# The last layer of a fused attention, expert and token-mixing kernel: token rows gathered as 512-byte quarters and transposed by VectorE, with GpSimd's elementwise work there given to VectorE

## The chip, the core and the metric

The kernel runs on one NeuronCore of a Trainium2 chip. The metric is the device time of one execution in microseconds (us). A core has TensorE (matrix products; PE and, for its weight loads, PEld in the profile), VectorE (DVE), ScalarE (ACT), GpSimd (POOL) and SyncE (SP, which here issues transfers). Each engine works through its own queue in order and waits on semaphores of the others. On-chip memory is SBUF and, for matrix results, PSUM; both have 128 partitions.

## What is computed

Three stages: attention with a local window, a mixture of 8 experts, and a last layer that mixes channels and tokens. Only the last one is changed in its working; the experts' output rows change their order of columns.

```
# last layer: x is (2, 768, 512), the output of the experts
theta = x @ w_theta
zr, zi = x * cos(theta), x * sin(theta)
y = w_tok_r @ zr + w_tok_i @ zi          # over the 768 tokens, for each batch element
u = x + y
out = u + max(u @ w_ch, 0)
```

## The kernel before

All products of the last layer are made of three passes: an operand is split into a high part, rounded for TensorE's faster 32-bit form (`F32R`), and the rest, and high by high, high by low and low by high are added in PSUM.

The experts (the loop over `u`, lines 1630 to 1724) write weighted rows to a table `yd` in device memory, in the order of expert slots: `y_rows` and `y_head` with ScalarE, `y_last` with VectorE, `y_few` with ScalarE. `first_put` builds block 0 of the next layer's transposed input by TensorE out of gathered rows and the last expert's rows.

The last layer (from line 1727) goes through 12 blocks of 128 tokens, 6 for each batch element. For block `k` these steps exist:

- `gather_y(k)` (L1736): GpSimd issues one indirect transfer that fetches the 128 rows, 2 KB each, into a tile `yg` (tokens on partitions). Four such buffers exist.
- `h_tr(k)` (L1747): TensorE transposes the four 128 by 128 squares into PSUM (tile `b`).
- `h_xh` (L1754) and `h_xf` (L1761): ScalarE copies that to `xh` (high part) and to `xTf`, the full transposed input that `u = x + y` needs at the end. `h_xl` (L1767): VectorE makes the low part `xl`.
- `h_theta(k)` (L1783): 12 matmuls of `xh` and `xl` with `wth`, into `th`.
- `trig_a` (L1793 to L1801): ScalarE and VectorE bring `th` into the range of the sine; `trig_s` (L1808 to L1810): ScalarE makes sin and, by half the angle squared, cos.
- `trig_b`: `si * x` on GpSimd (L1815), and on VectorE `kk = 1 - 2 kk` (L1821) and `kk * x` (L1822), with `x` the gathered rows.
- `trig_c`: ScalarE makes the high parts `z` (L1834); the low part of the sine side on GpSimd, of the cosine side on VectorE (both L1839). Block 0 and 1 use VectorE for all of it.
- `h_mix(k, d)` for d = 0 to 3 (L1859): 12 matmuls each, `z` with the token weights `wtok`/`wtokr`, summed over blocks into `a`.

The order is written out by hand: round `k` of the loop at line 1992 issues mix(k,0), gather(k+4), theta(k+2), transpose(k+3), mix(k,1), then trig_a(k+2) with the high and low part of x(k+3), trig_s, mix(k,2), trig_b, mix(k,3), trig_c. So TensorE is two blocks behind the gathering and one ahead in theta. Between these steps `job_tick` slips in pieces of a decoding job for weights (L401 to L414, ScalarE and VectorE); the last of 26 such jobs falls in round 7. At the end of a batch element (k = 5 and 11) `h_u` (L1871, L1878) adds the mixed sums to `xTf`, `h_split` (L1885, L1886) splits the result, with two of the four low parts of the first element on GpSimd, and `h_out` (L1896, L1904) makes the output.

Of the kernel before, what the change touches and what calls it, by code (L numbers as in the profile page):

```python
# [48 lines left out]
YLAST = RBASE[E - 1] * 128  # L49
NRAW = 3  # L50
# [35 lines left out]
HU = 32  # L86
XL = 0
# [8 lines left out]
def f32(ap):  # L96
    return ap.bitcast(F32)


@with_exitstack  # L100
def kernel(
# [93 lines left out]
    yidx = ct([128, NB], I32, "yidx")  # L195
    erows = {}
# [249 lines left out]
    with ExitStack() as actx:  # L446
# [338 lines left out]
        def lead_out():  # L785
            A.activation(y0, head["y"], AF.Copy)
# [582 lines left out]
    with ExitStack() as mctx:  # L1369
# [14 lines left out]

        def gather_p0():
            pslot[0] = mb.tile([128, 1], F32, tag="ps", name="ps", bufs=6)
            G.indirect_dma_start(pslot[0], None, pd[:], bass.IndirectOffsetOnAxis(ap=prow[:, 24:25], axis=0))
# [167 lines left out]
        def mm2_few(u, out=None):  # L1555
# [4 lines left out]
            for v in (u, u + 1):  # L1560
                hx, w = fews.pop(v)
                for g in range(128 // c if c < 128 else 0):
# [3 lines left out]
                        rhs=w[:, 4 * g * c : 4 * (g + 1) * c],  # L1566
# [22 lines left out]
        def y_rows(r, lo, hi):  # L1589
            for i in range(lo, hi):  # L1590
# [6 lines left out]
                A.activation(yo[:P, :W], yp[:P, :W], AF.Copy, scale=ps)  # L1597
# [13 lines left out]
        def y_few():  # L1611
# [8 lines left out]
            A.activation(yo, out[:, :W], AF.Copy, scale=pslot.pop(RBASE[E - 1] + 1))  # L1620
# [9 lines left out]
        for u in range(64):  # L1630
# [79 lines left out]
            if 0 <= i < RTILES[r]:  # L1710
                gather_p(r, i)
            if u == HU:
# [14 lines left out]
    with ExitStack() as hctx:  # L1727
        hb = hctx.enter_context(tc.tile_pool(name="hb", bufs=2, side="right", reuse_waits="tile"))
        pA = hctx.enter_context(tc.tile_pool(name="pA", bufs=6, space=PSUM))
        x2s, xTb, zs, xps, xparts, ths, trig, acc, us = {}, {}, {}, {}, {}, {}, {}, {}, {}  # L1730
# [7 lines left out]

        def h_tr(k, pool=None):
# [3 lines left out]
            if t == 0:  # L1743
                xTb[b] = hb.tile([128, 4, S], F32, tag="xTf", name="xTf")
            tp = (pool or pB).tile([128, 4, 128], F32, tag="a" if pool else "b", name="b")
            for j in range(4):
                PE.transpose(tp[:, j], x2s[k][:, j * 128 : (j + 1) * 128], ident)  # L1747
            xps[k] = tp

        def h_xh(k, both=True):  # L1750
# [5 lines left out]
            if both:  # L1756
# [28 lines left out]
        def trig_a(k, c=slice(0, DM), tick=lambda: None):  # L1785
# [9 lines left out]
            V.tensor_scalar(kk, kk, MAGIC, None, op0=ALU.subtract)  # L1795
# [16 lines left out]
        def trig_i(k, c=slice(0, DM), eng=G):  # L1812
            if k < NB:
                si = trig[k][2][:, c]
                eng.tensor_tensor(si, si, x2s[k][:, c], op=ALU.mult)  # L1815

        def trig_r(k, c=slice(0, DM)):
            if k >= NB:
                return
            kk, x2 = trig[k][0][:, c], x2s[k][:, c]  # L1820
            V.tensor_scalar(kk, kk, -2.0, 1.0, op0=ALU.mult, op1=ALU.add)  # L1821
            V.tensor_tensor(kk, kk, x2, op=ALU.mult)  # L1822

        def trig_b(k, c=slice(0, DM), eng=G):
# [16 lines left out]
        def trig_c(k, c=slice(0, DM), eng=G):  # L1841
# [145 lines left out]
        gather_y(4)  # L1987
# [4 lines left out]
        for k in range(1, NB):  # L1992
# [10 lines left out]
            gather_y(k + 4)  # L2003
# [12 lines left out]
            if k == HS:  # L2016
                h_split(0, 0, 0, S)
                h_split(0, 1, 0, S, G)
# [10 lines left out]
            if k == HS:  # L2029
                h_split(0, 2, 0, S)  # L2030
                h_split(0, 3, 0, S, G)
# [72 lines left out]
```

## Time and profile before

| | us |
|---|---|
| median of the 3 runs (474.62 to 477.23) | 474.84 |
| the profiled execution's own time | 472.97 |
| its span, first to last instruction | 471.2 |
| TensorE busy in the span | 462.9 (98%) |
| VectorE busy | 349.4 (74%) |
| ScalarE busy | 254.3 (54%) |
| GpSimd busy | 134.0 (28%) |

[...] The last layer lies between about 292 us and the end. The profile's views are: busy time by stretch, groups of instructions by line, the timeline, and the chain of work that ended last. In the timeline two instructions of one engine may overlap, since the next one starts while the one before drains.

### The profile page before, as it was taken

To read this page: it belongs to the slowest core of one execution; us is meant where nothing else is said; L and a number is where in the kernel's file an instruction comes from. 1 tells how busy PE (TensorE), PEld (TensorE's weight loads), DVE (VectorE), ACT (ScalarE), POOL (GpSimd) and SP (SyncE) were. 2 spreads that over 40 slices of the span, in tenths; PEclk is the share of its full clock that TensorE was granted. 3 is DMA by queue.
4 is the path that set the end of the run, shared out by engine and by line. 5 is a ranking of instruction groups with operands and counts; after the bars stand their busy time and mean duration, and the time that the engine had idled before them with its cause. 6 is when DMAs were issued, how large, how long until landed. Compare 5 with 4: busy or idle time off the path is not lost.

```text
span 471.2 us, 9456 instructions
## 1 busy us (share of the span) xinstructions
PE 462.9 (98%) x3310; PEld 382.6 (81%) x3310; DVE 349.4 (74%) x918; ACT 254.3 (54%) x613; POOL 134.0 (28%) x185
## 2 busy tenths in 40 slices
PE   8999999999999999999999999999999999999996
PEld 4677777788888898878777888888888888888885
DVE  5888889778678687878887746587999899751522
ACT  5988786722647666565754544556555355520300
POOL 8602322204041403040514302104543332430400
PEclk9999999999999999999999999999999999999999
DMA  8977577616967888888999991600023000001022
GB/s 243 370 226 255 166 250 248 231 47 197 323 181 232 281 292 272 256 255 275 310 348 298 304 321 61 207 24 22 24 73 125 12 19 19 1 33 35 34 79 93
DMA packets 60490, 82.97 MB, mean 176 GB/s; under 512 B 5608, under 2 KB 39656, under 8 KB 60440
## 3 DMA queue, kind: packets, MB, share of 16 engines
q1 hardware_dynamic: 52212, 62.06, 40.3%
q0 software_dynamic: 4272, 9.92, 6.7%
q10 hardware_dynamic: 3956, 10.36, 6.6%
q8 instruction: 27, 0.44, 0.4%
q14 instruction: 23, 0.19, 0.1%
HBM read 70.94 MB, written 11.38 MB: 175 GB/s over the span
## 4 chain that ended last, share of the span: by engine, by line
PE 86%; ACT 4%; DMA 3%; issue 3%; DVE 3%; POOL 1%; DVEq 0%; ACTq 0%; POOLq 0%
PE a L1859 21%; PE o L1547 12%; PE h L1474 8%; PE h L1491 8%; PE b L1896 7%; PE th L1783 7%; PE s L557 4%; PE x L636 3%; PE pt L612 3%; PE o L1563 2%; ACT pr L589 2%; DMA yd<-yo 2%; PE y L653 1%; PE tr L1323 1%; PE small L860 1%
## 5 line engine op out<-in xcount | busy, mean ns | idle before, releaser
L1859 PE MATMUL a<-wtokr,z 128*128 128x512 f32 x480 | 85.9, 337 | 0.0
L1859 PEld LDWEIGHTS a<-wtokr,z 128*128 128x128 f32 x480 | 73.8, 188 | 9.3
L1547 PE MATMUL o<-w2s,hh 128*128 128x512 f32 x192 | 62.9, 407 | 0.0
L589 ACT ACTIVATE pr<-sm,st 128x256 f32<-128x256 f32 (+1 forms) x96 | 46.0, 482 | 15.4 <-DVE st L579 15.3
L1491 PE MATMUL h<-xT,w1s 128*128 128x288 f32 (+3 forms) x384 | 51.9, 284 | 1.2 <-DVE w1s L1352 0.7
L1491 PEld LDWEIGHTS h<-xT,w1s 128*128 128x128 f32 x384 | 48.8, 189 | 4.4 <-DVE w1s L1352 1.1
L1456 DVE TENSOR_TENSOR w2s<-raw,w2s 128x512 fp32r<-128x512 f32 x56 | 38.4, 688 | 8.4 <-ACT w2s L1455 8.4
L579 DVE CUSTOM_DVE_ANT_0 sm<-s,bias 128x256 f32<-128x256 f32 (+1 forms) x96 | 34.0, 395 | 9.2 <-PE s L557 5.1
L1474 PEld LDWEIGHTS h<-xT,raw 128*128 128x128 f32 x256 | 37.0, 190 | 4.4 <-issue 3.9
L1474 PE MATMUL h<-xT,raw 128*128 128x192 f32 (+3 forms) x256 | 40.5, 311 | 0.0
L1547 PE MATMUL o<-w2s,hl 128*128 128x512 f32 x96 | 38.0, 396 | 0.0
L1547 PEld LDWEIGHTS o<-w2s,hh 128*128 128x128 f32 x192 | 32.3, 184 | 6.2 <-DVE w2s L1456 1.6
L1455 ACT ACTIVATE w2s<-raw 128x512 fp32r<-128x512 f32 x56 | 35.0, 628 | 2.9 <-DMA raw<-in_w_dram 1.4
L1599 POOL DMA_DIRECT2D yd<-yo x13 | 8.3, 636 | 80.3 <-ACT yo L1597 80.3
L1904 DVE SCALAR_TENSOR_TENSOR ob<-b,xTf 128x512 f32<-128x512 f32 (+1 forms) x16 | 8.8, 556 | 27.1 <-PE b L1896 24.3
L1815 POOL TENSOR_TENSOR si<-si,yg 128x512 f32<-128x512 f32 x10 | 13.5, 1346 | 50.5 <-ACT si L1808 47.5
L1352 DVE TENSOR_TENSOR w1s<-raw,w1s 128x512 fp32r<-128x512 f32 x32 | 21.9, 688 | 5.9 <-ACT w1s L1351 4.5
L557 PE MATMUL s<-kall,q 64*128 64x256 f32 (+1 forms) x192 | 26.2, 393 | 0.0
L411 ACT ACTIVATE wtokr<-jw 128x512 fp32r<-128x512 f32 x15 | 9.5, 633 | 29.4 <-DVE jw L408 29.4
L404 DVE SCALAR_TENSOR_TENSOR jw<-jraw,jw 128x512 int32<-128x512 int32 x26 | 24.7, 952 | 0.4
L406 DVE SCALAR_TENSOR_TENSOR jw<-jraw,jw 128x512 int32<-128x512 int32 x26 | 24.6, 948 | 0.2
L612 PE MATMUL pt<-ident,pr 128*128 128x128 f32 x176 | 24.6, 278 | 0.1
(289 smaller groups left out, 968.9 us busy)
## 6 DMA issues: line engine op xcount, KB each, us to landing
raw<-in_w_dram SPq DMA_DIRECT2D x60, 512.0 KB, 5.2
vv<-in_pack_dram SPq DMA_DIRECT2D x10, 512.0 KB, 5.5
jraw<-in_w_tokT_dram ACTq DMA_DIRECT2D x10, 512.0 KB, 4.5
w<-in_w_dram SPq DMA_DIRECT2D x16, 256.0 KB, 6.0
kall<-in_pack_dram SPq DMA_DIRECT2D x10, 320.0 KB, 5.0
xd<-xt SPq DMA_DIRECT2D x12, 256.0 KB, 2.2
q<-in_pack_dram SPq DMA_DIRECT2D x11, 256.0 KB, 4.4
jraw<-in_w_tokT_dram ACTq DMA_DIRECT2D x10, 256.0 KB, 4.8
```

What stands on the lines that cost most here:

```text
L557: PE.matmul(sp[hh][:, 0:W], lhsT=qs[n][half, j], rhs=kall[half, b, j, t * 160 + 160 - W : t * 160 + 160], start=True, stop=True,)
L579: V.tensor_tensor_reduce(out=sm[:, hh, 0:W], in0=ust[u]["s"][hh], in1=bias[:, 2 * j + hh], scale=-0.125, scalar=BIG, op0=ALU.add, op1=ALU.min,
L589: A.activation(pr[:, hh, 0:W], sm[:, hh, 0:W], AF.Exp, bias=st[:, hh : hh + 1], scale=-1.0, accum_out=sums[n][:, 2 * j + hh : 2 * j + hh + 1],
L612: PE.transpose(pt[:, hh, c], pr[:, hh, c * 128 : (c + 1) * 128], ident)
L1455: A.activation(h2, bb[:, o], AF.Copy)
L1456: V.tensor_tensor(l2, bb[:, o], f32(h2), op=ALU.subtract)
L1474: PE.matmul(hp[:, :N], lhsT=pieces[u // 2][1][:, j, o * 128 : (o + 1) * 128], rhs=x[:, j, :N], start=(j == 0), stop=(j == 3),)
L1491: PE.matmul(hp[:, :N], lhsT=wa[:, j], rhs=xa[:, j, :N], start=(k == 0), stop=(k == 11))
L1547: PE.matmul(out[:M], lhsT=ha[:, lo : lo + M], rhs=wa, start=(f == 0 and q == 0), stop=(f == 7 and q == 2),)
L1783: PE.matmul(th, lhsT=xa[:, j], rhs=wa[:, j], start=(n == 0), stop=(n == 11))
L1859: PE.matmul(acc[b][d][o], lhsT=za[:, d * 128 : (d + 1) * 128], rhs=wa[:, lo:hi], start=(t == 0 and n == 0 and (o == 0 or d % 2 == 0)), sto ...
L1896: PE.matmul(op[:, : hi - lo], lhsT=wa[:, d, e * 128 : (e + 1) * 128], rhs=ua[d][:, lo:hi], start=(n == 0), stop=(n == 11),)
```

## The change

For blocks 4 to 11 the transposed input no longer comes from TensorE. The columns of the rows in `yd` are put in another order ("woven": element 4c + j of a row is feature 128j + c), so that a quarter of a row, 512 bytes, holds 32 values of c with all four j. `gather_q(k)` fetches the block a second time, by four indirect transfers of 128 such quarters (tile `xq`), with quarter q of a token on partition group q; one VectorE transpose in 32 by 32 squares then writes the block's part of `xTf` directly. From there `xh` and `xl` are made as before. `gather_y(k)` still fetches the same rows whole, for the products with sin and cos, and is issued a round later. Both tiles share the four buffers of `yg`.

Who reads or writes woven rows changes its access: the writers of `yd` write with a step of 16 bytes; the products `si * x` and `kk * x`, the transposes of blocks 1 to 3 and the weight loads of `first_put` read with it; the few-token matmuls of the experts read four runs of `w` instead of one. The default engine of `trig_i`, `trig_b` and `trig_c` and two `h_split` calls turn from GpSimd to VectorE, and L1795's subtraction turns from VectorE to ScalarE for blocks 4 on. `piece_rows` (four times 4 small VectorE instructions during the experts) works out the quarters' row numbers.

```diff
+        def piece_rows(q):
+            for i in range(4):
+                V.tensor_scalar(yq[32 * q : 32 * q + 32, i], yidx[32 * i : 32 * i + 32, VT:NB], 4.0, float(q), op0=ALU.mult, op1=ALU.add)
...
-                        lhsT=rows[:, j * 128 : (j + 1) * 128],
+                        lhsT=woven(rows)[:, j],
...
-                        rhs=w[:, 4 * g * c : 4 * (g + 1) * c],
+                        rhs=plain(w)[:, :, g * c : (g + 1) * c],
...
-                A.activation(yo[:P, :W], yp[:P, :W], AF.Copy, scale=ps)
+                A.activation(woven(yo[:P, :W]), yp[:P, :W].rearrange("p (j c) -> p j c", j=4), AF.Copy, scale=ps)
...
-            V.tensor_scalar(yo, yps[E - 1][0], pslot.pop(RBASE[E - 1]), None, op0=ALU.mult)
+            V.tensor_scalar(woven(yo), plain(yps[E - 1][0]), pslot.pop(RBASE[E - 1]), None, op0=ALU.mult)
...
+        def gather_q(k):
+            if not VT <= k < NB:
+                return
+            xq = xqs[k] = hb.tile([128, DM], F32, tag="yg", name="xq", bufs=4)
+            for i in range(4):
+                G.indirect_dma_start(
+                    xq[:, i * 128 : (i + 1) * 128],
+                    None,
+                    yd.rearrange("n (q w) -> (n q) w", q=4),
+                    bass.IndirectOffsetOnAxis(ap=yq[:, i, k - VT : k - VT + 1], axis=0),
+                )
...
+            if k >= VT:
+                xps[k] = xTb[b][:, :, t * 128 : (t + 1) * 128]
+                V.transpose(
+                    xps[k].rearrange("p j (i a) -> p i j a", i=4),
+                    xqs.pop(k).rearrange("p (i c j) -> p i j c", i=4, j=4),
+                )
+                return
...
-                PE.transpose(tp[:, j], x2s[k][:, j * 128 : (j + 1) * 128], ident)
+                PE.transpose(tp[:, j], woven(x2s[k])[:, j], ident)
...
-            V.tensor_scalar(kk, kk, MAGIC, None, op0=ALU.subtract)
+            if k < VT:
+                V.tensor_scalar(kk, kk, MAGIC, None, op0=ALU.subtract)
+            else:
+                A.activation(kk, kk, AF.Copy, bias=-MAGIC)
...
-        def trig_b(k, c=slice(0, DM), eng=G):
+        def trig_b(k, c=slice(0, DM), eng=V):
...
-        def trig_c(k, c=slice(0, DM), eng=G):
+        def trig_c(k, c=slice(0, DM), eng=V):
...
-            gather_y(k + 4)
+            gather_q(k + 4)
+            if k + 3 >= VT:
+                gather_y(k + 3)
...
-                h_split(0, 1, 0, S, G)
+                h_split(0, 1, 0, S)
```

VectorE's queue in the last layer, one round of a block (round 4; `jw` and `jraw` are the decoding job's, `z` the split sine and cosine products), before:

```order
L1797 SCALAR_TENSOR_TENSOR rr<-kk,th 128x512
L1799 SCALAR_TENSOR_TENSOR rr<-kk,rr 128x512
L1801 TENSOR_SCALAR rr<-rr 128x512
L1767 TENSOR_TENSOR xl<-b,xh 128x512
L402 TENSOR_SCALAR jw<-jraw 128x512
L404 SCALAR_TENSOR_TENSOR jw<-jraw,jw 128x512
L1821 TENSOR_SCALAR kk<-kk 128x512
L1822 TENSOR_TENSOR kk<-kk,yg 128x512
```

The same round after, in the changed kernel's own line numbers, with `xq` the quarters:

```order
L1792 STREAM_TRANSPOSE xTf<-xq 128x4x4x32
L1852 SCALAR_TENSOR_TENSOR rr<-kk,th 128x512
L1854 SCALAR_TENSOR_TENSOR rr<-kk,rr 128x512
L1856 TENSOR_SCALAR rr<-rr 128x512
L1819 TENSOR_TENSOR xl<-xTf,xh 128x512
L419 TENSOR_SCALAR jw<-jraw 128x512
L421 SCALAR_TENSOR_TENSOR jw<-jraw,jw 128x512
L1873 TENSOR_TENSOR si<-si,yg 128x512
L1879 TENSOR_SCALAR kk<-kk 128x512
```

The transpose stands ahead of the round's first reduction step, the sine product ahead of L1879 (L1821 before), `xl` now reads two SBUF tiles, and the subtraction of L1795 is gone. GpSimd's queue where the last layer begins (`pfew` is a small gather of the experts), before:

```order
L1393 DMA pfew<-pd,sidx 128x1
L1517 MEMSET y_107 128x2x16
L1736 DMA yg<-yd,yidx 128x512 x4
L1815 TENSOR_TENSOR si<-si,yg 128x512
L1839 TENSOR_TENSOR z_4680<-si,z_4679 128x512
```

and after:

```order
L1422 DMA pfew<-pd,sidx 128x1
L1546 MEMSET y_107 128x2x16
L1768 DMA yg<-yd,yidx 128x512 x3
L1777 DMA xq<-yd,Lall 128x128 x8
L1768 DMA yg<-yd,yidx 128x512
```

From there GpSimd holds transfers alone until the end of the second batch element, four of quarters and one of whole rows in turn, in place of a transfer, a product and a low part; the quarters' row numbers lie in `Lall`'s memory.

## Rows read from the trace of the kernel before

**Rows 1.** The page: busy time, share of the span and instructions of TensorE.
```profile
PE 462.9 (98%) x3310; PEld 382.6 (81%) x3310; DVE 349.4 (74%) x918; ACT 254.3 (54%) x613; POOL 134.0 (28%) x185
```
**Rows 2.** By stretch: length, then busy us of PE, PEld, DVE, ACT, POOL; clock, DMA.
```profile
200.00:292.00 92.00, 91.59 (x605) 73.79 (x604) 69.50 (x148) 51.32 (x104) 24.41 (x34) 1.00 0.84 279
326.40:338.00 11.60, 11.60 (x66) 10.06 (x65) 11.17 (x17) 6.85 (x13) 5.00 (x4) 1.00 0.08 23
```
**Rows 3.** The chain that ended last: start, length, engine, tile, line, count.
```profile
349.78 2.79 PE th L1783 x12
353.01 8.33 PE a L1859 x48
...
407.61 2.79 PE th L1783 x12
410.40 6.25 PE a L1859 x36
```
**Rows 4.** Timeline of VectorE, first instruction of two rounds: start, length, line.
```profile
324.52 0.42 DVE L1795 TENSOR_SCALAR kk<-kk 128x512 f32<-128x512 f32 x1
...
334.36 0.42 DVE L1795 TENSOR_SCALAR kk<-kk 128x512 f32<-128x512 f32 x1
```
**Rows 5.** One line of the decoding job on VectorE, whole kernel: shortest/median/longest ns.
```profile
L404 DVE SCALAR_TENSOR_TENSOR jw<-jraw,jw x26: 678/688/1678, 19.3 to 392.4; 128x512 int32<-128x512 int32 x26
```
**Rows 6.** Groups of the last layer by shape: count, busy us, mean ns, idle before.
```profile
L1839 POOL TENSOR_TENSOR z<-si,z 128x512 fp32r<-128x512 f32 x10 | 16.5, 1648 | 8.7 <-ACT z L1834 8.7
L1815 POOL TENSOR_TENSOR si<-si,yg 128x512 f32<-128x512 f32 x10 | 13.5, 1346 | 50.5 <-ACT si L1808 47.5 <-PE a L1859 2.9
...
L404 DVE SCALAR_TENSOR_TENSOR jw<-jraw,jw 128x512 int32<-128x512 int32 x7 | 11.7, 1673 | 0.2
L406 DVE SCALAR_TENSOR_TENSOR jw<-jraw,jw 128x512 int32<-128x512 int32 x7 | 11.4, 1630 | 0.0
...
L1822 DVE TENSOR_TENSOR kk<-kk,yg 128x512 f32<-128x512 f32 x7 | 4.8, 692 | 0.2
```
**Rows 7.** Timeline around theta of block 4: VectorE, and TensorE's weight loads.
```profile
321.67 0.94 DVE L1839 TENSOR_TENSOR z<-kk,z 128x512 fp32r<-128x512 f32 x1 [0.76 <-ACT z L1834]
...
326.76 0.68 DVE L1767 TENSOR_TENSOR xl<-b,xh 128x512 fp32r<-128x512 f32 x1
...
328.12 0.89 PEld L1783 LDWEIGHTS th<-wth,xl 128*128 128x128 f32 x4
```
**Rows 8.** Timeline around theta of block 8, at the first batch element's end.
```profile
370.10 0.68 DVE L1767 TENSOR_TENSOR xl<-b,xh 128x512 fp32r<-128x512 f32 x1
...
374.38 0.89 PEld L1783 LDWEIGHTS th<-wth,xl 128*128 128x128 f32 x4
```
**Rows 9.** Sums over eight on VectorE by line; the first steps 36 bytes.
```profile
L237 DVE TENSOR_REDUCE Lall<-lh x12: 277/283/287, 18.4 to 99.7; 128x9 f32<-128x72 f32 x12
...
L800 DVE TENSOR_REDUCE rank<-cmp x1: 220/220/220, 106.2 to 106.2; 128x8 f32<-128x64 f32 x1
...
L844 DVE TENSOR_REDUCE slotf<-sl x1: 353/353/353, 110.5 to 110.5; 128x24 f32<-128x192 f32 x1
```
**Rows 10.** Lines whose access turns to 16-byte steps: shortest/median/longest ns.
```profile
L1439 PEld LDWEIGHTS first<-ident,rows x8: 187/192/192, 289.3 to 290.2; 128*128 128x128 f32 x8
...
L1597 ACT ACTIVATE yo<-o,ps x15: 368/672/694, 148.8 to 280.1; 128x512 f32<-128x512 f32 x9, 128x128 f32<-128x128 f32 x2, 128x256 f32<-128x256 f32 x2, 112x512 f32<-112x512 f32 x1
```
**Rows 11.** GpSimd's gathers in the timeline, and a VectorE step beside one.
```profile
294.54 0.95 POOL L1736 DMA_INDIRECT yg<-yd,yidx  x1 [0.30 <-issue]
...
295.80 0.95 POOL L1736 DMA_INDIRECT yg<-yd,yidx  x1 [0.30 <-issue]
...
331.84 1.27 POOL L1736 DMA_INDIRECT yg<-yd,yidx  x1
...
332.36 0.69 DVE L408 SCALAR_TENSOR_TENSOR jw<-jm,jw 128x512 f32<-128x512 f32 x1
```
**Rows 12.** By line: landing of L1736's gathers; small VectorE copies of the experts.
```profile
DMA to landing us min/median/max: 3.3/3.6/5.0
...
L1411 DVE COPY sidx<-toks x16: 131/144/149, 129.5 to 284.4; 32x1 int32<-32x1 int32 x12, 64x1 int32<-64x1 int32 x4
```

More of the change, by code (lines that the diff above doesn't have):

```diff
@@ L49 @@
 YLAST = RBASE[E - 1] * 128
+VT = 4
 NRAW = 3
@@ L86 @@
 HU = 32
+QIDX = (50, 52, 54, 56)
 XL = 0
@@ L97, in f32, with woven, plain @@
     return ap.bitcast(F32)
+def woven(ap):
+    return ap.rearrange("p (c j) -> p j c", j=4)
+def plain(ap):
+    return ap.rearrange("p (j c) -> p j c", c=128)
 @with_exitstack
@@ L195 @@
     yidx = ct([128, NB], I32, "yidx")
+    yq = Lall.rearrange("p k e -> p (k e)")[:, 0 : 4 * (NB - VT)].bitcast(I32).rearrange("p (i k) -> p i k", i=4)
     erows = {}
@@ L785, in lead_out @@
         def lead_out():
-            A.activation(y0, head["y"], AF.Copy)
+            A.activation(woven(y0), plain(head["y"]), AF.Copy)
         cp = rt([128, 2, 8], "cp")[:, 0]
@@ L1383, in width @@
             return 32 if M <= 32 else 64 if M <= 64 else 128
+        def piece_rows(q):
+            for i in range(4):
+                V.tensor_scalar(
+                    yq[32 * q : 32 * q + 32, i],
+                    yidx[32 * i : 32 * i + 32, VT:NB],
+                    4.0,
+                    float(q),
+                    op0=ALU.mult,
+                    op1=ALU.add,
+                )
         def gather_p0():
@@ L1619, in y_few @@
             yo = y0[:, 384 : 384 + W]
-            A.activation(yo, out[:, :W], AF.Copy, scale=pslot.pop(RBASE[E - 1] + 1))
+            ps = pslot.pop(RBASE[E - 1] + 1)
+            A.activation(woven(yo), out[:, :W].rearrange("p (j c) -> p j c", j=4), AF.Copy, scale=ps)
             SP.dma_start(groups_out(YLAST + 128, M, W), yo)
@@ L1711 @@
                 gather_p(r, i)
+            if u in QIDX:
+                piece_rows(QIDX.index(u))
             if u == HU:
@@ L1755, in h_xh @@
             xparts[k] = [xh]
-            if both:
+            if both and k < VT:
                 h_xf(k)
@@ L1810, in trig_s, with rows, trig_i @@
             A.activation(kk[:, c], kk[:, c], AF.Square)
-        def trig_i(k, c=slice(0, DM), eng=G):
+        def rows(k, c):
+            return woven(x2s[k])[:, c.start // 128 : c.stop // 128] if k else plain(x2s[k][:, c])
+        def trig_i(k, c=slice(0, DM), eng=V):
             if k < NB:
                 si = trig[k][2][:, c]
-                eng.tensor_tensor(si, si, x2s[k][:, c], op=ALU.mult)
+                eng.tensor_tensor(plain(si), plain(si), rows(k, c), op=ALU.mult)
         def trig_r(k, c=slice(0, DM)):
@@ L1819, in trig_r @@
                 return
-            kk, x2 = trig[k][0][:, c], x2s[k][:, c]
+            kk = trig[k][0][:, c]
             V.tensor_scalar(kk, kk, -2.0, 1.0, op0=ALU.mult, op1=ALU.add)
-            V.tensor_tensor(kk, kk, x2, op=ALU.mult)
-        def trig_b(k, c=slice(0, DM), eng=G):
+            V.tensor_tensor(plain(kk), plain(kk), rows(k, c), op=ALU.mult)
+        def trig_b(k, c=slice(0, DM), eng=V):
             trig_i(k, c, eng)
@@ L1986 @@
         h_mix(0, 3)
-        gather_y(4)
+        gather_q(4)
         trig_a(2)
@@ L2030 @@
                 h_split(0, 2, 0, S)
-                h_split(0, 3, 0, S, G)
+                h_split(0, 3, 0, S)
             if HS < k < HS + 4:
```

3 lines of the change are left out of this document (2 added, 1 removed).

## The prediction

> **What bounds the kernel now.** I read the page first, then busy time by stretch, then the chain that ended last, and last the timeline of the rounds that change. The page has TensorE busy for 98% of the span [rows 1]. By stretch it is busy for all of a round of the last layer, 11.60 of 11.60 us, and nearly all of the experts, 91.59 of 92 us, at full clock; VectorE is close behind in the round, 11.17 us [rows 2]. The chain agrees: it runs on TensorE alone, theta then mix then theta, without a wait. A hole stands between the two where a block is transposed: theta of block 6 ends at 349.78 + 2.79 = 352.57 and mix begins at 353.01. Where no block is transposed, theta of block 11 ends at 410.40 and mix begins at 410.40 [rows 3]. So TensorE's own work sets the end, and anything taken out of it counts while VectorE and ScalarE keep feeding it. How near VectorE is to not doing so: its rounds take 334.36 - 324.52 = 9.84 us [rows 4] against TensorE's 11.56 (theta to theta, 349.78 to 361.34, that is 2.79 + 0.44 + 8.33). It is ahead, by 1.7 us a round more.
>
> **The transposes removed.** Eight blocks lose their four transposes, each 0.44 us on the path [rows 3]: 8 x 0.44 = 3.5 us. Nothing else on TensorE moves. This is the whole gain; GpSimd's freed time is worth nothing by itself, since no step of the chain waits for it.
>
> **VectorE's round.** It takes in the transpose, the sine product and the sine low part, and gives up the subtraction L1795. The two moved steps have a row, 0.69 us for two inputs [rows 6]; that the next instruction may start while one drains I leave out, which makes the additions a little too dear. The subtraction gives back 0.42 [rows 4]. The transpose has no row; the nearest ones, 128x512 from SBUF to SBUF on VectorE, are 0.42 for one input and 0.69 for two [rows 4, 6]. I take 0.69, the dearer of the two, with 0.42 and, below, 1.08 as ends. [...] Against these three additions stands a relief: beside GpSimd's products (1.35 and 1.65 us each) the job's steps L404 and L406 take 1.67 and 1.63 us [rows 6], while L404's median over the kernel is 0.69 [rows 5]. With GpSimd's products gone both should fall to 0.69, 0.98 + 0.94 = 1.9 us. Round after: 9.84 - 0.42 - 1.9 + 3 x 0.69 = 9.6 us, against 11.56 - 0.44 = 11.1 for TensorE. The cover stays about as it is, 1.5 us a round.
>
> **Where the cover is thin: block 4.** VectorE is late only once. `xl` of block 4 is made from 326.76 to 327.44 and TensorE loads it at 328.12, 0.68 us later [rows 7]. TensorE will now be there 0.44 earlier, since block 4's transposes, ahead of that mix, are gone. On VectorE a transpose is set in (0.69), the product and low part of block 2 are set in ahead, mostly in its waits for ScalarE, and L1839 loses the 0.25 us it pays beside GpSimd (0.94 [rows 7] against 0.69 for a two-input step [rows 6]). Net 0.44 later against 0.24 of cover left: a wait of 0.2 us, once; with a product and a transpose 0.39 dearer each, 1.0. I take 0.4. Afterwards the cover regrows. At the first batch element's end VectorE has the additions of `h_u` on top; there `xl` of block 8 is ready at 370.78 and needed at 374.38, 3.6 us later [rows 8], and the extra steps of two rounds there are paid by the relief of two rounds. No wait.
>
> **Sixteen-byte steps.** Woven rows make VectorE read and ScalarE write with a step of 16 bytes, and TensorE load weights so. A step of 8 bytes is free: L404 reads every other word and takes 0.688 [rows 5], like a plain two-input step at 0.692 [rows 6]. A step of 36 bytes is not: L237 sums 72 elements in 283 ns, L800 64 contiguous ones in 220, L844 192 in 353 [rows 9]. The contiguous slope is 133 / 128 = 1.04 ns, so 72 would take 228, and the step costs 55 / 72 = 0.76 ns an element, 0.39 us on 512. So one such instruction costs between 0 and 0.39 us more. Sixteen lies nearer to 8 and I take the lower third, 0.1: 0.3 us a round on VectorE (two products and the transpose), under the cover of 1.5. For TensorE no strided load stands in the trace; `first_put` has 16 weight loads (eight for each of its two sources [rows 10]) and blocks 1 to 3 twelve, so with 0 to 0.10 us (128 x 0.76 ns) each the bound is 0 to 2.8 us on the path. I take 0.4, again near the lower end. ScalarE's 15 writes [rows 10] are 0 to 0.39 each, beside a TensorE that waits for 0.4 us in 92 [rows 2]: 0, at most 0.5. The few-token matmuls read runs of 32 words or more: 0.
>
> **The rest.** GpSimd issues five gathers a round, 1.26 us apart [rows 11], 6.3 of 11.1 us, with 3.6 us to land [rows 12]; SyncE's queue is not touched. Quarters of a block wait only for the transpose two blocks ahead and are wanted a round later; hidden. If a gather were late, VectorE's queue would stop at the transpose, with the reduction and `xl` behind it. The subtraction on ScalarE replaces the copy to `xTf`, one ScalarE step for another. `piece_rows` is 16 instructions like the 0.14 us copies [rows 12], 2.3 us on a VectorE that is busy for 69.5 of 92 there [rows 2]: 0, at most 0.5. The half additions and splits at the end of the first element gain more from GpSimd's silence than they add.
>
> **The sum.** -3.5 + 0.4 (block 4) + 0.4 (strided loads) = -2.7 us. The profiled execution becomes 472.97 - 2.7 = 470.3; that execution lies 1.87 below the median of the runs, 474.84, which the same sum brings to 472.1.
>
> **Rivals.** *Every 16-byte step pays the 36-byte price.* For it: L237 is the only strided row beyond 8 bytes, and it pays on each element. Against it: 16 is not 36, and the row at 8 pays nothing. VectorE's round is then 9.6 + 3 x 0.39 = 10.8, still under 11.1; block 4 waits 1.0, the loads cost 2.8, ScalarE's writes 0.5: -3.5 + 4.3 = +0.8, so 475.6, no change. [...]
>
> *VectorE becomes the bound (slower).* The point is 1.5 us more a round: from 0.5 us extra on each of the two products and the transpose, VectorE sets the pace in the seven rounds with jobs. At twice the plain length, with 0.69 extra on each of the three, 2.1, the rounds lose 0.6 each, 4.2, block 4 waits 1.5, the loads cost 2.8: -3.5 + 8.5 = +5.0, 479.8. For it: no row shows the transpose. Against: every plain 128x512 row on VectorE is near 0.69 where GpSimd is still [rows 5].
>
> *The relief fails,* because GpSimd's gathers hold VectorE as its products did: the round is 9.6 + 1.9 = 11.5, 0.4 over TensorE's; seven rounds lose 2.8, block 4 waits 0.5, the loads cost 0.4: -3.5 + 3.7 = +0.2, 475.0, no change. Against it: L408 beside a gather, at 332.36, keeps its 0.69 [rows 11].
>
> **How the numbers follow.** Forecast 472.1 (471.2 to 473.2): 0.50. All steps pay: 475.6 (474 to 477.5): 0.28. VectorE bound: 0.14. Relief fails: 0.08. About 0.5%, 2.4 us, is what a measurement here can tell from no change. Faster by more means under 472.5: most of the forecast, 0.42, and a little of the rest: 0.44. Slower by more means over 477.2: the bound case and the edge of the second: 0.18. Between: 0.38. The range takes the forecast and the second case: 470.8 to 477.5.
>
> **What would show it.** TensorE's rounds at 11.1 us and theta running into mix without the 0.44 hole; L404 and L406 at 0.69; VectorE's rounds of work at 9 to 10; one short wait of TensorE for `xl` of block 4 and no other; the transpose near 0.7; strided products at 0.7 to 0.8; weight loads of `first_put` still 0.19 long. Products near 1.1, or longer gaps between the loads of blocks 1 to 3, speak for the second case; TensorE waiting for `xl` or `z` every round for the third. The forecast is wrong if gathers land late or TensorE waits anywhere in the experts.

## The result: slower, partly in the work and partly behind it

The changed kernel takes 479.27 us (median of 20 runs, 475.60 to 480.50), the kernel before 474.61 (20 runs, 473.53 to 479.31). The ratio is 1.0076, with a 95% interval of 1.0055 to 1.0098; a second measurement (e0, below) gave 479.41 against 474.26, 1.0091 (1.0067 to 1.0116). So the change costs 0.5 to 1.2%. Forecast was 472.1, faster, with a range that ended at 477.5.

The profiled execution took 479.62 us by its own clock, with a span of 473.8. Before it was 472.97 and 471.2. So between these two executions 2.6 us came in the span, and what lies around the span grew from 1.8 to 5.8 us. The execution profiled before was a quick one, 1.6 us under its median, so 2.6 is the high end for the span: by the medians of e0 the span grew by 1.7 us, and the rest came behind it. These are two losses. First the span. The page of the changed kernel (its lines answer to [rows 1]):

```profile
PE 461.3 (97%) x3277; PEld 381.0 (80%) x3278; DVE 359.5 (76%) x956; ACT 262.4 (55%) x613; POOL 134.9 (28%) x195
...
PE 65%; DVE 16%; ACT 7%; issue 6%; DMA 4%; POOL 1%; ACTq 0%; DVEq 0%; POOLq 0%
```

TensorE has 1.6 us less to do, yet VectorE, ScalarE and DMA now hold shares of the chain that ended last. By line (shortest/median/longest ns), the steps whose access turned to 16 bytes, and the decoding job's two steps:

```profile
L1792 DVE STREAM_TRANSPOSE xTf<-xq x8: 1080/1087/1101, 328.4 to 404.2; 128x512 f32<-128x512 f32 x8
...
L1873 DVE TENSOR_TENSOR si<-si,yg x12: 608/1079/1103, 313.2 to 419.9; 128x512 f32<-128x512 f32 x10, 128x256 f32<-128x256 f32 x2
...
L1880 DVE TENSOR_TENSOR kk<-kk,yg x12: 621/1086/1093, 314.1 to 421.5; 128x512 f32<-128x512 f32 x10, 128x256 f32<-128x256 f32 x2
...
L1636 DVE TENSOR_SCALAR yo<-o,ps x1: 1126/1126/1126, 290.0 to 290.0; 128x512 f32<-128x512 f32 x1
...
L1626 ACT ACTIVATE yo<-o,ps x15: 487/1190/1222, 148.4 to 280.2; 128x512 f32<-128x512 f32 x9, 128x128 f32<-128x128 f32 x2, 128x256 f32<-128x256 f32 x2, 112x512 f32<-112x512 f32 x1
...
L1468 PEld LDWEIGHTS first<-ident,rows x8: 308/329/329, 290.6 to 292.2; 128*128 128x128 f32 x8
...
L421 DVE SCALAR_TENSOR_TENSOR jw<-jraw,jw x26: 678/689/748, 19.0 to 397.9; 128x512 int32<-128x512 int32 x26
...
L423 DVE SCALAR_TENSOR_TENSOR jw<-jraw,jw x26: 640/684/947, 22.4 to 401.0; 128x512 int32<-128x512 int32 x26
```

Every one of these strided steps is dear: the product `kk * x` 1.09 us against 0.69 [rows 6], ScalarE's writes 1.19 against 0.67, the loads of block 0 0.33 against 0.19 [rows 10]. The relief came in full: no step of the job is longer than 0.95 us where two took 1.6 [rows 6].

Where the last layer begins, the chain reads (start, length, what):

```profile
278.62 1.11 ACT yo L1626
...
280.22 0.52 ACT yo L1626
...
280.76 5.14 DMA yd<-yo
...
286.67 3.86 DMA rows<-yd,yidx
...
290.66 3.97 PE first L1468 x16
```

Before, this stretch was TensorE's alone. Now the chain runs from the write of `yo` over its transfer to the gather of block 0's rows, for which TensorE waits 0.7 us, and its 16 loads then take 3.97 us (2.00 before, 289.69 to 291.69 in the same view). The wait for the rows is not the steps' doing for certain: e0, the same kernel, has none there, while e11 and e14 below, which write rows without 16-byte steps, wait 0.4 and 0.7 us for the same rows. The longer loads stand in every trace that has them: from the first of these 16 matmuls to the `few` matmuls behind block 0's theta 7.2 to 7.4 us pass in the eight traces with strided loads and 5.5 to 5.7 in eleven without (6.0 in e17, with 0.3 of it a wait). The strided loads cost 1.6 to 1.9 us there.

ScalarE's longer writes cost TensorE something earlier, in the experts. Behind such a write ScalarE has to round the next weights, `w1s`, and TensorE waits for these (timeline from 200 us to 206 us, before and then after):

```profile
200.78 0.69 ACT L1597 ACTIVATE yo<-o,ps 112x512 f32<-112x512 f32 x1
201.35 0.64 ACT L1351 ACTIVATE w1s<-raw 128x512 fp32r<-128x512 f32 x1
```
```profile
200.93 1.22 ACT L1626 ACTIVATE yo<-o,ps 112x512 f32<-112x512 f32 x1
201.91 0.67 ACT L1368 ACTIVATE w1s<-raw 128x512 fp32r<-128x512 f32 x1
...
202.63 0.36 PE L1520 MATMUL h<-xT,w1s 128*128 128x208 f32 x1 [0.45 <-ACT w1s L1368]
```

This wait, 0.44 to 0.47 us long at 202 us to 204 us, stands in all nine traces of this study with 16-byte writes and in none of the other eleven.

Theta of block 1 starts 3.0 us late (timeline, before and then after):

```profile
299.91 2.13 PE L1783 MATMUL th<-wth,xh 128*128 128x512 f32 x8
```
```profile
302.93 2.14 PE L1835 MATMUL th<-wth,xh 128*128 128x512 f32 x8
```

Of TensorE's waits from 286 us to 425 us these are listed (total, times, longest); before the change the list is empty:

```profile
PE a L1917 <- DVE xTf L1929: 1.1, 1, 1.1
PE th L1835 <- ACT xh L1806: 0.8, 1, 0.8
PE first L1468 <- DMA rows<-yd,yidx: 0.7, 1, 0.7
```

The second is block 4, with 0.4 more for `xl` behind it; the first is the end of the first batch element, where the mix of the second needs PSUM that `h_u` on VectorE has yet to read. Between the two the chain runs on VectorE, which is busy for 10.0 of 10.3 us a round:

```profile
339.05 1.00 DVE xTf L1792
340.06 0.58 DVE rr L1852
...
343.58 1.07 DVE si L1873
...
345.02 1.08 DVE kk L1880
...
349.31 1.01 DVE xTf L1792
```

That is 10.26 us from transpose to transpose, 0.9 under TensorE's new round: VectorE is late at block 4 and catches up, until `h_u` comes on top. TensorE's round is 11.12 where nothing waits (theta of blocks 9 and 10):

```profile
387.73 2.79 PE th L1835 x12
390.52 8.33 PE a L1917 x48
398.86 2.79 PE th L1835 x12
401.65 8.33 PE a L1917 x48
409.98 2.79 PE th L1835 x12
```

Theta of block 11 starts at 409.98 against 407.61 [rows 3]: 3.1 late at the start (theta of block 3), 3.5 won by eight transposes, 2.8 lost again: 1.2 at block 4, 1.3 at the end of the first element, 0.3 in small pieces.

Behind the span, the DMA view from 475 us to 480 us of the changed kernel shows five fetches of code, after the last instruction at 473.8 (queues: packets, MB, share):

```profile
q14 instruction: 4, 0.03, 1.7%
q8 instruction: 1, 0.02, 1.6%
```

Before, no packet moves after 471.2. Runs of the changed kernel lie either 1.8 to 1.9 us above their span (7 of 20) or 4.5 to 5.8 (13 of 20); the kernel before lay 1.8 to 2.0 above in all 107 runs that were made beside the experiments.

### The profile page after: what moved, and what is told of

It is laid out like the page before. It is cut to its first block, busy times and chain, and to the rows that moved or that the text cites. A ratio compares the mean times of both kernels' runs of the same rounds, so it can differ in the third digit from the quotient of the medians.

```text
span 473.8 us, 9431 instructions
## 1 busy us (share of the span) xinstructions
PE 461.3 (97%) x3277; PEld 381.0 (80%) x3278; DVE 359.5 (76%) x956; ACT 262.4 (55%) x613; POOL 134.9 (28%) x195
## 4 chain that ended last, share of the span: by engine, by line
PE 65%; DVE 16%; ACT 7%; issue 6%; DMA 4%; POOL 1%; ACTq 0%; DVEq 0%; POOLq 0%
PE a L1917 11%; PE o L1576 9%; PE b L1954 7%; PE h L1503 7%; PE h L1520 6%; PE s L574 4%; PE x L653 3%; PE pt L629 3%; DMA yd<-yo 3%; PE th L1835 2%; ACT pr L606 2%; PE o L1592 2%; PE h L783 2%; DVE kk L1880 2%; PE y L794 2%
## 5 line engine op out<-in xcount | busy, mean ns | idle before, releaser
L1777 POOL DMA_INDIRECT xq<-yd,Lall x32 | 33.7, 1054 | 44.0 <-DVE xTf L1792 20.0
L653 PE MATMUL x<-ps,vv 128*64 128x128 f32 x352 | 24.5, 279 | 0.0
L1835 PE MATMUL th<-wth,xh 128*128 128x512 f32 x88 | 22.6, 398 | 0.8 <-ACT xh L1806 0.8
```

The source lines that it names most:

```text
L653: PE.matmul(xp[64 * hh : 64 * hh + 64, j], lhsT=vv[:, i, h * 64 : (h + 1) * 64], rhs=ps[:, hh, c], start=(c == 0), stop=(c == nch - 1),)
L1777: G.indirect_dma_start(xq[:, i * 128 : (i + 1) * 128], None, yd.rearrange("n (q w) -> (n q) w", q=4), bass.IndirectOffsetOnAxis(ap=yq[:, i ...
```

## The experiments

The span is given as the median over the runs, that of the kernel before from runs beside them on the same chip; "behind" counts runs with 4.4 us or more between span and time. In e1, e2, e3 and e17 columns of x meet the wrong rows of the weights, and e16 doesn't transpose: these five serve for the time alone.

| run | time | before | span | before | behind |
|---|---|---|---|---|---|
| e0 the change | 479.41 | 474.26 | 474.1 | 472.4 | 5 of 6 |
| e1 no steps | 472.55 | 472.92 | 467.7 | 471.1 | 12 of 12 |
| e2 steps on VectorE | 475.43 | 472.92 | 470.1 | 471.1 | 6 of 6 |
| e3 steps in writers, loads | 476.30 | 472.92 | 471.1 | 471.1 | 8 of 10 |
| e17 steps in writers | 474.87 | 472.78 | 469.9 | 470.9 | 5 of 5 |
| e4 products moved | 472.60 | 472.92 | 470.8 | 471.1 | 0 of 12 |
| e6 e4 and gathers | 474.14 | 474.26 | 472.4 | 472.4 | 0 of 12 |
| e7 woven, TensorE transposes | 476.99 | 474.26 | 475.2 | 472.4 | 0 of 12 |
| e16 copies for transposes | 476.25 | 472.78 | 471.6 | 470.9 | 4 of 6 |
| e9 8-byte steps, 4 blocks | 476.85 | 474.34 | 471.4 | 472.5 | 5 of 5 |
| e10 8-byte steps, 6 blocks | 484.69 | 474.34 | 482.9 | 472.5 | 0 of 5 |
| e5 hint early | 476.39 | 474.26 | 474.2 | 472.4 | 1 of 7 |
| e11 before, no hint | 477.36 | 474.34 | 475.6 | 472.5 | 0 of 6 |
| e12 change, VectorE padded | 477.93 | 472.75 | 473.1 | 470.9 | 5 of 6 |
| e13 before, VectorE padded | 472.93 | 472.75 | 471.1 | 470.9 | 0 of 12 |
| e14 e9, VectorE padded | 474.90 | 472.75 | 469.1 | 470.9 | 5 of 5 |
| e15 before, transposes added | 473.05 | 472.78 | 471.2 | 470.9 | 0 of 11 |
| e18 change, TensorE padded | 496.91 | 472.62 | 492.5 | 470.8 | 5 of 6 |

**Are the steps the cause in the span?** Four kernels take them out in parts.

In writers and loads (e1 and e2; the other writers in the same way):

```diff
-A.activation(woven(yo[:P, :W]), yp[:P, :W].rearrange("p (j c) -> p j c", j=4), AF.Copy, scale=ps)
+A.activation(yo[:P, :W], yp[:P, :W], AF.Copy, scale=ps)
...
-lhsT=woven(rows)[:, j],
+lhsT=rows[:, j * 128 : (j + 1) * 128],
...
-PE.transpose(tp[:, j], woven(x2s[k])[:, j], ident)
+PE.transpose(tp[:, j], x2s[k][:, j * 128 : (j + 1) * 128], ident)
```

On VectorE (e1 and e3; the cosine side in the same way):

```diff
-xqs.pop(k).rearrange("p (i c j) -> p i j c", i=4, j=4),
+xqs.pop(k).rearrange("p (i j c) -> p i j c", i=4, j=4),
...
-eng.tensor_tensor(plain(si), plain(si), rows(k, c), op=ALU.mult)
+eng.tensor_tensor(si, si, x2s[k][:, c], op=ALU.mult)
```

> The changed kernel with every 16-byte step taken out: rows are written, loaded as weights, transposed and multiplied in runs of 128 or 32 words, so in blocks 4 to 11 the columns of x meet the wrong rows of the weights; every instruction, transfer and wait stays. If the steps are what costs (theory S), the last layer starts as in the kernel before (theta of block 1 near 300.0 us, against 302.9 in the changed kernel), the transpose and the two products take about 0.7 us instead of 1.08, TensorE waits nowhere for more than 0.3 us, and the span is 471.2 - 3.5 + 0.3 = 468.0 us. If the transpose and the moved work are too long whatever their step (theory T), the transpose stays near 1.08, the waits of TensorE before block 4 and at the first element's end (0.9 and 1.1 us) stay, and the span is 470 or more. The time lies 1.8 us above the span, or 5 to 6 where code is still loaded after the last instruction.

> The changed kernel with the 16-byte steps kept on VectorE alone (the transpose and the two products of each block); the writers of the rows, the weight loads of block 0 and the transposes of blocks 1 to 3 go in plain runs, so that the columns of blocks 0 to 3 and of the written rows don't belong together. Theory S: the start is as before the change (theta of block 1 near 300.0), VectorE's rounds stay at 10.3 us and TensorE waits as in the changed kernel, about 0.9 and 1.1 to 1.4 us: span 473.8 - 3.0 = 470.8. Theory T expects the same of the waits, and the start at 300.0 too; it differs from S in the run without any steps only. If the start is late because of the quarter gathers or the sixteen small index instructions and not because of the steps, theta of block 1 stays near 303 and the span near 473.8.

> The changed kernel with the 16-byte steps kept in the writers of the rows, the weight loads of block 0 and the transposes of blocks 1 to 3, and taken out of VectorE's transposes and products, which read runs of 32 and 128 words; columns of x then meet the wrong rows of the weights. Theory S: theta of block 1 near 302.9 as in the changed kernel, VectorE's round 10.3 - 1.2 = 9.1 us of work, no wait of TensorE over 0.3 us: span 473.8 - 2.4 = 471.4, no better than before the change. Theory T (the transpose is long whatever its step): waits stay, span 473 to 473.8.

In e1 TensorE waits for nothing from 286 us to 425 us, and the three VectorE steps are (view by line):

```profile
L1792 DVE STREAM_TRANSPOSE xTf<-xq x8: 701/704/706, 325.2 to 395.3; 128x512 f32<-128x512 f32 x8
...
L1873 DVE TENSOR_TENSOR si<-si,yg x12: 414/682/693, 310.8 to 412.0; 128x512 f32<-128x512 f32 x10, 128x256 f32<-128x256 f32 x2
...
L1880 DVE TENSOR_TENSOR kk<-kk,yg x12: 424/692/695, 311.6 to 413.7; 128x512 f32<-128x512 f32 x10, 128x256 f32<-128x256 f32 x2
```

So the transpose costs 0.70 us in plain runs, as the prediction had taken it, and 0.38 more by its step. Theory T falls. Against the kernel before beside them the spans are -3.4 without steps, -1.0 with those on VectorE, 0.0 with those in writers and loads: the two groups cost 2.4 and 3.4 us. Their sum with the -3.4 would be +2.4; e0 measured +1.7 and the profiled execution +2.6. In e2 TensorE waits as in the changed kernel:

```profile
PE a L1917 <- DVE xTf L1929: 1.1, 1, 1.1
PE th L1835 <- ACT xh L1806: 0.9, 1, 0.9
```

In e3 it waits for nothing in this stretch. So these two waits come with the steps on VectorE and go with them.

e17 is e3 with the loads plain as well:

> The kernel of e3 (steps in the writers of the rows and in TensorE's loads only) with the loads too in plain runs, so that the steps stay in the writers alone; the columns of x don't meet their weights. It parts the late start of 3.4 us (e3 against e1) into loads and writers. By the trace the 16 loads of block 0 take 3.8 us instead of 2.2 and the transposes of blocks 1 to 3 cost 0.45 more, 2.0 together; the writers make the last expert's rows late by 1.1: the span is 2.0 us under that of e3 and 1.1 to 1.4 over that of e1 against the kernel before, that is 2.0 to 2.3 under the kernel before; block 0 starts 1.1 late, theta of block 1 too.

By the spans it divides the 3.4 as 2.4 for the writers (its -1.0 against e1's -3.4) and 1.0 for the loads, from five to twelve runs each whose spans scatter by 2 us. The expectation had it the other way round, 1.1 to 1.4 and 2.0. The traces put the loads at 1.6 to 1.9, as said above; in e17 0.3 of that is lost again, since TensorE, sooner done with the first eight loads, waits for the rows that `y_last` writes with steps (1.13 us, 0.75 before). For the writers they show the 0.45 us behind `w1s` and these 0.3; where the rest of the 2.4 lies isn't shown, and e17's profiled execution, 1.4 us over its median, can't tell: its chain there begins with a transfer of weights (`late`, 11.4 us). What is shown is that the writers, which the prediction put at nothing, cost TensorE at least 0.45 us.

**Do the moved products, the gathers or the woven rows cost anything else?** e4 is the kernel before with `eng=G` turned to `eng=V` and the subtraction on ScalarE; e6 adds 32 quarter gathers; e7 is the change without quarters.

> The kernel before with one part of the change alone: GpSimd's products and low parts go to VectorE and the subtraction of blocks 4 on to ScalarE; rows plain, TensorE transposes all blocks. The relief as predicted: the decoding job's steps fall from 1.67 and 1.63 to 0.69 us beside the last layer, VectorE's round is about 9.2 us against TensorE's 11.56, no wait, span 471.2 within 0.3, time 474.6. If the moved work makes VectorE late by itself, TensorE waits at block 4 or at the first element's end and the span is 472 or more.

> The kernel of e4 (GpSimd's products on VectorE, TensorE's transposes kept) with 32 indirect transfers of 128 pieces of 512 bytes added, four a round, into two small tiles that nobody reads. It asks what the transfers alone do. If they bring the fetches of code after the end (a longer GpSimd queue, more descriptors to be set up again), the time lies 5 to 6 us above the span; if not, 1.8. In the span, if the transfers cost nothing by themselves, as the prediction had it, it stays at 470.5 to 471.2; if GpSimd's writing of descriptors holds up VectorE, VectorE's steps beside them grow over 0.69 us and the span by 1 us or more.

> The changed kernel without quarter gathers and without VectorE's transposes: rows woven, all writers and readers with 16-byte steps, TensorE transposes all blocks out of woven rows, GpSimd's work on VectorE. Theory S: the start is late by 3.1 us as in the changed kernel (theta of block 1 at 302.9), VectorE's round is 9.2 + 2 x 0.39 = 10.0 us against 11.56 of TensorE, so it waits nowhere; eight transposes of four strided weight loads add 0.03 to 0.4 us each on top: span 471.2 + 3.1 + 0.3 to 3 = 474.6 to 477.3. The distance from the time to the span tells whether the fetches after the end come with the rows' order (5 to 6) or with the gathers and VectorE's transposes (1.8).

e4 is no slower (1.0005, 0.9989 to 1.0021) and shows the relief by itself:

```profile
L404 DVE SCALAR_TENSOR_TENSOR jw<-jraw,jw x26: 681/693/709, 19.1 to 390.8; 128x512 int32<-128x512 int32 x26
...
L406 DVE SCALAR_TENSOR_TENSOR jw<-jraw,jw x26: 640/684/947, 22.5 to 393.1; 128x512 int32<-128x512 int32 x26
```

e6 is level too, and VectorE's job step L406 keeps its 0.69 us beside the gathers: they don't hold VectorE. e7 has the steps, but not the transposes' gain, and loses 2.8 us in the span.

In e16, further down, copies of 0.61 us take the place of the transposes of 1.09 (0.81 to 1.08 was expected): the wait at the end of the first element is gone, that for `xh` of block 4 falls from 0.8 to 0.4 us, and the span lies 0.7 over that of the kernel before, where e0 had 1.7. VectorE is so near to the pace that 0.5 us a round decides these waits.

**Can the steps be had free?** e9 weaves by two, 8 bytes, with two pieces of 256 bytes for each partition group, and transposes four blocks on VectorE; e10 six.

```diff
-    return ap.rearrange("p (c j) -> p j c", j=4)
+    return ap.rearrange("p (h c m) -> p h m c", h=max(1, ap.shape[-1] // 256), m=2)
...
-            if k >= VT:
+            if k in VB:
```

> A version that computes everything, with steps of 8 bytes in place of 16: rows woven by two (element 256h + 2r + m of a row is feature 128(2h + m) + r), so that a partition group needs two pieces of 256 bytes a token and a block eight transfers; blocks 5, 7, 9 and 11 alone are transposed by VectorE, since GpSimd's nine transfers a block take 9 x 1.25 = 11.3 us; the branch hint stands ahead of the last output's first part. If a step of 8 bytes is free, as the decoding job's 0.69 us says, the products stay at 0.69, the two half transposes take 0.4 each, weight loads of block 0 stay at 0.19 us, the start is not late (theta of block 1 within 0.7 us of the kernel before), TensorE waits nowhere, and four blocks give 4 x 0.44 = 1.8 us: span 1.5 to 1.9 under that of the kernel before in the same call, time the same. If 8 bytes cost a part of what 16 do, products 0.8 to 1.0 and the start 1 to 2 us late, the span is no shorter than before.

> The same with six blocks (5, 6, 7, 9, 10, 11) transposed by VectorE: 6 x 0.44 = 2.6 us less on TensorE. With four row buffers, nine transfers of 1.25 us and 3.6 us to land for each of two or three blocks in a row, quarters may come late: if GpSimd keeps up, the span is 2.4 to 2.7 under that of the kernel before; if not, VectorE stands at the transpose for them, TensorE waits for xh of blocks 6, 7, 10 and 11, 1 to 4 us each, and the span is at or over that of the kernel before.

The steps of e9 by line:

```profile
L1797 DVE STREAM_TRANSPOSE xTf<-xq x8: 398/417/438, 334.9 to 397.8; 128x256 f32<-128x256 f32 x8
...
L1885 DVE TENSOR_TENSOR kk<-kk,yg x12: 424/693/744, 312.4 to 416.2; 128x512 f32<-128x512 f32 x10, 128x256 f32<-128x256 f32 x2
...
L1628 ACT ACTIVATE yo<-o,ps x15: 378/717/743, 148.7 to 279.3; 128x512 f32<-128x512 f32 x9, 128x128 f32<-128x128 f32 x2, 128x256 f32<-128x256 f32 x2, 112x512 f32<-112x512 f32 x1
...
L1470 PEld LDWEIGHTS first<-ident,rows x8: 194/196/197, 289.5 to 290.4; 128*128 128x128 f32 x8
```

All are within 7% of plain runs but the transpose, which is two halves here (0.83 against 0.70). TensorE's own transposes are the exception: their loads take 0.20 us in e9 as with 16 bytes (0.21), against 0.14 in plain runs. The span falls by 1.1 us, and by 1.8, the whole of 4 x 0.44, in the padded e14. Yet the time of both is longer than before (1.0056 and 1.0041), for what lies behind the span. No version in this study that computes everything beats the kernel before in time. e10 is 10 us slower. Sixteen transfers for two blocks stand ahead of the rows of block 5 on GpSimd, which are fetched only at

```profile
337.28 0.95 POOL L1770 DMA_INDIRECT yg<-yd,yidx  x1 [0.30 <-issue]
```

But neither these rows nor the quarters, which the expectation had named, are what TensorE stands for. From 330.5 us to 340.7 us it goes through the end of block 4's theta and the first matmuls of the next mix one or a few at a time, with gaps of up to 1.7 us in which it waits for nothing that the profile shows (waits from 286 us to 430 us):

```profile
PE a L1922 <- issue: 4.9, 5, 1.7
PE th L1840 <- issue: 2.3, 3, 1.1
```

The products that read block 5's rows come only at 358 us. GpSimd issues the last six of these seventeen transfers in that stretch, and TensorE's granted clock is 0.73 to 0.76 from 331 us to 351 us (1.00 ahead of it and after, 0.989 over the span); what holds TensorE stays open.

**What brings the fetches behind the span?** Nine runs asked this.

> The changed kernel itself once more, beside the kernel before on one chip, to compare span with span and time with span. Expected of every theory: span 473.8 to 474.5, which is 2.6 us over the kernel before in the same call, and a time 5 to 6 us above the span in most runs and 1.8 in a few, while the kernel before lies 1.8 above its span throughout: +2.6 in the span, +2 to 4 behind it.

> The changed kernel with one thing moved: the hint on the branch around the unused general path, which stands between the two parts of the last output, stands ahead of the first part, some 15 us earlier. In the changed kernel five fetches of code begin 3.1 us after the last instruction, one per engine, and the time lies 5.8 us above the span. If these fetches are for that branch and the hint comes too late for them, an earlier hint takes them away and the time lies 1.8 us above the span, at 475.6; the span stays 473.8. If they have another cause, the time stays 5 to 6 us above the span in most runs.

> The kernel before with the branch hint taken out and nothing else. If the five fetches of code after the last instruction, which the changed kernel shows and the kernel before doesn't, are those of the branch around the general path when its hint has had no effect, they now appear here too, 2 to 3 us after the end of the span, and the time lies 4.4 to 5.8 us above the span in every run, span unchanged at 471 to 472.5. If the time stays 1.8 above the span, the fetches have nothing to do with that branch.

> The changed kernel with 30 empty VectorE steps (a fill of 128 words, one at the head of each of the first 30 steps of the experts' loop), so that VectorE's stream of instructions grows from 1186 to 1216 and all its later code moves by 30 places. Of the kernels so far, those with the fetches after the end have 1186 and 1202 instructions on VectorE, those without 1130 to 1169 and 1213; on no other engine do the counts part the two. If the place of VectorE's code decides it, the time lies 1.8 us above the span here, in all or nearly all runs, at 475.5 to 476.5, span 473.8 to 474.6 as before. If the transpose on VectorE or anything that the change does decides it, the time stays 4.5 to 5.8 above the span in most runs.

> The kernel before with 60 of the same empty steps, so that VectorE's stream grows from 1131 to 1191 instructions, between the two counts that had the fetches after the end. If the place of VectorE's code decides, they appear here, in a kernel that knows nothing of the change: time 4.5 to 5.8 us above the span in most runs, span 471 to 472.8. If not, the time stays 1.8 above the span.

> The version with steps of 8 bytes and four blocks on VectorE (e9), with 20 of the same empty steps: 1222 instructions on VectorE instead of 1202. If the place of VectorE's code decides, the time lies 1.8 us above the span, and with e9's span of 471.4, 1.1 us under that of the kernel before, the time is 473.2 and about 0.25% under that of the kernel before. If not, it stays at 476.5.

> The kernel before with eight VectorE transposes added, one of 128x512 in plain 32 by 32 squares behind the last step of each of blocks 4 to 11, into a tile that is free by then; nobody reads the result. If a VectorE transpose in the program is what brings the code fetches after the end, the time lies 4.5 to 5.8 us above the span in most runs here; if not, 1.8. In the span nothing is expected: VectorE's round grows by 0.7 us from 9.84 to 10.5, under TensorE's 11.56, so it stays within 0.4 us of the kernel before.

> The changed kernel with its eight transposes replaced by plain VectorE copies of the same tiles and the same 16-byte steps, so that blocks 4 to 11 are not transposed and their part of the result is wrong; all else stays. If the transposes bring the fetches after the end, the time lies 1.8 us above the span, else 4.5 to 5.8. The copies with 16-byte steps cost 0.42 + 0.39 to 0.66 us, 0.81 to 1.08; the span stays within 1 us of the changed kernel's.

> The changed kernel with 45 empty matmuls of one column on TensorE ahead of a small transpose of the last expert, so that TensorE's stream is again as long as that of the kernel before (the profile lists 3442 loads and waits there, 3397 in the changed kernel) and its code of the last layer's end stands at the old place. If the place of TensorE's code decides on the fetches after the end, the time lies 1.8 us above the span in all or nearly all runs; if not, 4.5 to 5.8 in most. The empty matmuls themselves cost 45 x 0.06 to 0.19 us on TensorE, so the span grows by 3 to 9 us and isn't compared.

The edits are a line or two each. e5 moves the hint, and e11 takes it out of the kernel before:

```diff
-            if part[0]:
+            if not part[0]:
```

e12 pads the experts' loop (with 60 in e13, in the kernel before, and 20 in e14, in e9):

```diff
+            if u < 30:
+                V.memset(slot0, 0.0)
```

e15 adds a transpose behind `trig_c(k + 2)` of the kernel before, e16 puts `V.tensor_copy` for `V.transpose`, and e18 pads `first_hitT`:

```diff
...
+                V.transpose(kk.rearrange("p (i a) -> p i a", a=32), rr.rearrange("p (i a) -> p i a", a=32))
```
```diff
+            for _ in range(45):
+                PE.matmul(tp[:, 1, 0:1], lhsT=ident, rhs=ident[:, 0:1], start=True, stop=True)
```

The early hint took the fetches away in 6 of 7 runs, which looked like the answer; but the kernel before without any hint has none (it loses 3.1 us inside the span instead), and e9 and e14 carry the early hint and have them in every run. The place of VectorE's code fell, for the shifts tried, with e12 and e13, the transpose with e15 and e16, gathers alone with e6, woven rows with e7. e18 is weaker than planned: each empty matmul stands as two loads in its trace, so that TensorE's stream came 45 instructions past its old length instead of level with it, and the place of TensorE's code isn't ruled out. What is left is a coincidence: each kernel that shows them leaves blocks to quarter gathers instead of TensorE's transposes, and of those kernels only e10 shows none. The cause stays open. What is shown is that they and the longer time go together: of the 20 traces, the eleven whose time lies 4.7 us or more above the span have five or six fetches after the last instruction, and the nine at 1.8 to 1.9 have none. Their price is 2.7 to 4 us in most runs of the changed kernel. For which engine each fetch is, the views don't tell.

## Why the prediction was wrong

- **What bounds the kernel, and the gain** were right: TensorE, and 8 x 0.44 = 3.5 us; e1, which keeps all else, gained 3.4 in the span.
- **The relief** was right: 0.69 us for both steps, e4 level. The rival of gathers that hold VectorE fell with e6.
- **The transpose** at 0.69: right for plain runs (0.70). With the 16-byte step it takes 1.09, at the upper end that the prediction named, 1.08.
- **The failed step: sixteen-byte steps.** The prediction had a free row at 8 bytes and a dear one at 36 [rows 9], called 16 nearer to 8 and took 0.1 of 0 to 0.39 us. Measured are +0.39 on a product and +0.38 on the transpose, that is the upper end to the hundredth; on a write by ScalarE +0.52, over the bound of 0.39, which came from VectorE. Distance on the axis of bytes was no reason. On VectorE and in ScalarE's writes the step turned dear between 8 and 16 bytes: a product takes 0.69 us with 8 (e9) and 1.09 with 16, against 0.69 in plain runs, a write 0.72 and 1.19 against 0.67.
- **ScalarE's writes at 0, cover unnamed.** The term was "0, at most 0.5". TensorE's busy time had room for nothing [rows 2], and the writes were put beside it without looking at what ScalarE does next. The prediction's own sign came, a wait of TensorE in the experts: 0.45 us for `w1s` behind a write, in every trace with such writes. By the spans of e1 and e17 the writers together cost 2.4 us, `y_last` on VectorE among them, which had no term at all; the traces place about a third of that.
- **Loads** at 0.4, bounds 0 to 2.8: by the traces 1.6 to 1.9 us for block 0 and 0.1 to 0.2 more for blocks 1 to 3; by the spans of e3 and e17 1.0. Inside the bounds, toward the upper end. One load of block 0 costs 0.14 us more, over the 0.10 that the bound was made of.
- **Block 4's wait** at 0.4, 1.0 if products and transpose are 0.39 dearer: 1.2 measured. The place was right.
- **No wait at the first element's end** was wrong. The prediction looked there at `xl` of block 8 alone [rows 8]; what came late is PSUM that `h_u` frees, 1.3 us.
- **The rival "every 16-byte step pays"** was the right one, with its price at +0.8; in the span the change has +1.7 to +2.6. It lacked the wait at `h_u` and had the writers at 0.5. VectorE's round, forecast at 10.8 in it, was 10.3, so the rival in which VectorE becomes the bound is not what happened, though its 479.8 lies near the measured 479.27: VectorE is late twice and faster than TensorE in between.
- **What lies around the span** was put at no change without a reason: the sum counts work in the span and was taken off the time. (The 1.87 us in it are the distance of the profiled execution from the median; between its span and its time lay 1.8.) This grew by 4.0 in the profiled execution and by 3.0 to 3.5 in the medians, and it is what put the time outside the range: without it the changed kernel would have been at 476.2 (its median span of 474.4 and 1.8), inside the range and near the 475.6 of the rival. No row of before shows it, and its cause stays open.

## To carry to other kernels

Between a free stride and a dear one, don't interpolate: take the dear end until a row stands on the stride itself. When a writer gets slower, look at what its engine does next and who waits for that, and follow the written data to its next reader, however idle the engine is on average. And compare the span with the kernel's own time in every run, since a change can cost as much behind the last instruction as in the work.

## What the runs showed of the hardware beyond this

- A step of 16 bytes in 32-bit data costs by kind of instruction, on 128x512: two inputs on VectorE 0.69 to 1.09 us, a transpose 0.70 to 1.09, a plain copy only to 0.61 (e16; one-input steps of this size take 0.42 [rows 4]), a ScalarE write 0.67 to 1.19. The same with 8 bytes: 0.69, 2 x 0.42 for the transpose, and 0.72 for the write. TensorE's 128x128 loads differ by their use: 0.19, 0.20 and 0.33 us plain, with 8 and with 16 bytes for block 0's, 0.14, 0.20 and 0.21 for those of its transposes.
- VectorE's transposes move 128x512 values in 32 by 32 squares in 0.70 us in plain runs (e1), the time of a two-input step, 0.69 [rows 6].
- Code can be fetched after a kernel's last instruction, and where it is the time is 2.7 to 4 us longer; whether it happens differs from run to run of one program (in 13 of 20 by the time).
- One-column matmuls of 32-bit data aren't small: the 45 of e18 took 16.6 us, twice the upper end expected, as 90 passes of 0.18 us each with a load of its own. The granted clock in that stretch (288.5 to 305 us) was 0.59, and 0.76 in the 7 us behind it, against 1.00 in the experts of the kernel before [rows 2]:

```profile
288.47 16.58 PE L1461 MATMUL tr<-ident 128*128 128x1 f32 x90
```
